# First layers of two MLPs: seven products of 128 rows and one of 64 in place of eight of 120

## The chip, the cores and the metric

The kernel runs on one core of a Trainium2 chip. The metric is the device time of one execution in microseconds (us), as the median of several runs. Beside the runs there is one profiled execution, from which all rows below are taken. The engines are named as in the profile: PE is TensorE (PEld its weight loads), DVE is VectorE, ACT is ScalarE, POOL is GpSimd, SP is SyncE, whose queue issues the DMA transfers.

## What is computed

A linear-attention recurrence over 768 steps for 4 x 8 heads of 40 elements, and behind it two MLPs on the 3072 resulting tokens of 320 elements, each with 2048 hidden elements. The MLPs are dense (one set of weights for all tokens).

```python
def _attn_ref(r, k, v, w, a, b):
    for t in range(S):                      # S = 768, state is (4, 8, 40, 40)
        y[:, :, t] = np.einsum('bhd,bhde->bhe', rt, state)
        Sa = np.einsum('bhde,bhe->bhd', state, at)
        state_decay = state * wt[:, :, None, :] - np.einsum('bhd,bhe->bhde', Sa, bt)
        state = state_decay + np.einsum('bhd,bhe->bhde', vt, kt)

def _moe_ref(x, w_in, w_out):               # x (3072, 320), w_in (320, 2048), w_out (2048, 320)
    h = x @ w_in
    g = h * np.cos(h)
    return g @ w_out

def _moe2_ref(x, w_in, w_out, s, b):
    h = x @ w_in
    r = np.maximum(h, 0.0)
    g = s * (r * r) + b
    return g @ w_out
```

## The kernel before

**Chunks.** Time is cut into 12 chunks of 64 steps. A chunk gives 4 x 64 = 256 tokens. For each chunk `prep` (L1164) loads and scales the inputs, `chain` (L1190) carries the state on, `yt` (L984) leaves the attention's output as two f16 parts (high and low, `yhl`), `xs` (L1009) writes these to DRAM and `x1_load` (L1016) reads them back with the elements of a token on the partitions. `mlp` (L1198) then runs the first MLP on the chunk. When all attention is done, the second MLP runs over the 12 chunks: `x2` (L1063) loads a chunk of the first MLP's result, splits it into high and low parts and transposes it on TensorE.

**Numbers in two parts.** Every f32 operand of the MLPs is a sum of two f16 numbers, high and low. A product of x and w is x_hi w_hi + x_lo w_hi + x_hi w_lo.

**The first layer.** The 320 elements of a token are laid out as 120 + 120 + 80 rows. The 80 rows that are left take 40 more rows from the low parts, so that the tile `w1` (and `w2`), [120, 16, 6, 128], holds six stationary operands for each of the 16 blocks of 128 hidden elements: two high, two low, and two that mix the last 80 high rows with 40 rows of low ones. `first` (L1020) issues eight products for each block `ff`, 120 rows x 128 columns stationary, 256 tokens moving, all into one half of a PSUM bank `hp`. `m1_f` (L1026) and `m2_f` (L1081) call it for ff = 2p and 2p+1, and issue the activation (Sin, Relu) and its split into `gh` and `gl` directly behind the second. `m1_s` and `m2_s` are the second layer: for a pair p and a half m of the tokens, six products of 320 columns into a bank `op`.

**Order.** `mlp` records, for each p, `f(p,0)`, `s(p-2,0)`, `f(p,1)`, `s(p-2,1)`. All operations go through a planner (`Recorder`, L96) that knows each operation's cost and successors; it emits for every engine the operation that can start first, and of equals the one with the longest work behind it. Successive TensorE products of one recorded step are one operation for it. It keeps at most two `hp` and two `op` banks live, and six for attention, of the eight that PSUM has ("cls", L1219). Its cost for products that use at most 64 rows is half of that for more (`cost`, L164); it knows no cost of changing from one kind to the other. All emitted instructions carry line 407, so rows are told apart by the tiles' names.

**Weights.** `weights` (L620) loads `w1` in 16 pieces as 8-byte words; `w_in_chunk` (L575) turns them into f32 on DVE, into the f16 high part on ACT (two operations, as the last 80 rows are wanted twice), and into the low part on POOL. The 40-row pieces of the low part (`wlo`) are moved to rows 80 to 119 by two small transfers for each pair of blocks (`w_in_pair`, L564). `w2` is loaded in 8 pieces of twice the size after attention. `place` (L540) puts raw words into parts of `w1` and `v1` that are not filled yet. The tests (`w_in_test`, `norm`) square the weights and sum them up, as part of a check of the range of numbers.

**Names in the rows.** hp and op are the two layers' banks; tsp are f16 transposes of 40 rows, in turn from rows 0 to 39 and 64 to 103; UD is a product of one row and 512 columns; dtp<-UN,up are f32 products on 32 x 32 pieces, each call two instructions; txp and xtp are transposes of 128 rows; vraw and wraw are raw weights.

Of the kernel before, what the change touches and what calls it, by code (L numbers as in the profile page):

```python
# [29 lines left out]
HEADS = [0, 3, 6, 1, 4, 7, 2, 5]  # L30
# [416 lines left out]
class Fast:  # L447
# [73 lines left out]
    def norm(self, rows, sq, i, k=0):  # L521

        nc = self.nc
        ps = self.pp.tile([128, 2], F32, tag="at", bufs=8, name="np")
        for j, x in enumerate(sq):
            nc.tensor.matmul(ps, x, rows[0:x.shape[0]], start=(j == 0), stop=(j == len(sq) - 1))
        nc.vector.tensor_reduce(out=self.norms[:, k, i:i + 1], in_=ps, axis=AX.X, op=ALU.max)
# [11 lines left out]
    @staticmethod  # L539
    def place(dst, k):  # L540

        q = k + 3 if k < 5 else k if k < 8 else k - 2 if k < 10 else None
        if q is not None:
            return dst[:, 2 * q:2 * q + 2].rearrange("p f a n -> p (f a n)").bitcast(U64)

    def w_in_load(self, src, dst, k):
        p, tag, raws, n = self.wtags[:4]
        raw = self.place(dst, k) if n == 128 else None
        if raw is not None:
            raw = raw.rearrange("p (a n) -> p a n", a=3)  # L550
        else:
            raw = p.tile([120, 3, n], U64, tag=tag, bufs=raws, name="wraw")
        self.RAW["i", k] = raw
        self.nc.sync.dma_start(out=raw, in_=src[:, :, k * n:k * n + n])

    def w_out_load(self, src, dst, k):
        p, tag, raws, n = self.wtags[:4]
        raw = self.place(dst, k) if n == 128 else None
# [5 lines left out]
    def w_in_pair(self, dst, name, k):  # L564

        nc = self.nc
        p, _, _, n, tag, bufs = self.wtags
        lo = p.tile([80, 2, 128], F16, tag=tag, bufs=bufs, name="wlo")
        m = n // 128
        for i in range(0, 2, m):  # L570
            self.w_in_chunk(dst, name, k * 2 // m + i, n, lo[:, i:i + m])
# [3 lines left out]
    def w_in_chunk(self, dst, name, k, n, lo):  # L575
        nc = self.nc
        raw = self.RAW["i", k]
        st = self.float32(raw)
        m = n // 128
# [5 lines left out]
        nc.gpsimd.tensor_tensor(out=wv[:, 2:4], in0=sv[:, 0:2], in1=wv[:, 0:2], op=ALU.subtract)  # L585
        nc.gpsimd.tensor_tensor(out=lo, in0=sv[0:80, 2], in1=wv[0:80, 4], op=ALU.subtract)
# [11 lines left out]
    def w_in_test(self, src, name, k):  # L598

        nc = self.nc  # L600
        sq = self.pm.tile([120, 2, 3, 128], BF16, tag="xs", name="wsq", bufs=4)
        for i, (rows, a, n) in enumerate(((120, 0, 2), (80, 4, 1))):
            nc.scalar.activation(sq[0:rows, :, 2 * i:2 * i + n], src[0:rows, 2 * k:2 * k + 2, a:a + n], AF.Square, scale=1.0 / SW,
                                 accum_out=self.st[0:rows, STAT_IX[name], 2 * k + i:2 * k + i + 1])
        if name == "w1":
            for f in range(2):
                self.norm(self.ones, [sq[0:j, f, i] for i, j in enumerate((120, 120, 80))], 2 * k + f, 1)
# [12 lines left out]
    def weights(self, wn, vn, wd, vd):  # L620
        for k in range(0, NFF, 2):
            l = [(self.w_in_load, self.i[wn], wd, k), (self.w_in_load, self.i[wn], wd, k + 1), (self.w_in_pair, wd, wn, k // 2)]
            for j in (k, k + 1):
                l += [(self.w_out_load, self.i[vn], vd, j), (self.w_out_chunk, vd, vn, j)]
            for j, f in enumerate(l):
                self.do(*f)
                self.nc.base[self.nc.blk] = 265 - 2 * k if j < 3 else 200 - 3 * k
# [356 lines left out]
    def yt(self, c, pg):  # L984
# [12 lines left out]
        if pg == 0:  # L997
            self.Y[c] = self.pa.tile([128, 9, 2, 2 * C], F16, tag="yhl", name="yhl", bufs=1)
# [3 lines left out]
        nc.scalar.activation(self.Y[c][:, 8, pg], y[:, 2 - pg], AF.Copy)  # L1002
# [4 lines left out]
        self.norm(self.halves, [sq[:, h] for h in range(4)], 2 * c + pg)  # L1007

    def xs(self, c):  # L1009

        nc = self.nc
        for hf in range(2):
            y = self.Y[c][hf * 64:hf * 64 + 40].rearrange("p (j i) k t -> p j (i k t)", j=3)
            nc.sync.dma_start(out=self.x0[c, hf].rearrange("j p n -> p j n"), in_=y)

    def x1_load(self, c):  # L1016
        x = self.XS[c] = self.pm.tile([120, 2, 6, 128], F16, tag="xs", name="xs", bufs=4)
        self.nc.sync.dma_start(out=x, in_=self.x0[c].rearrange("f j p n -> (j p) f n"))

    def first(self, ps, w, x, ff):  # L1020
        for i, (a, b) in enumerate(((0, 0), (0, 1), (1, 2), (1, 3), (2, 0), (3, 2), (4, 4), (5, 5))):
            self.nc.tensor.matmul(ps, w[:, ff, a], x[:, b // 2, b % 2], start=(ff % 2 == 0 and i == 0), stop=True,
                                  skip_group_check=True)


    def m1_f(self, c, p, k):  # L1026
        nc = self.nc
        if k == 0:
            self.HP[p] = self.ph.tile([128, 2, TB], F32, tag="at", bufs=8, name="hp")
        ps, x = self.HP[p], self.XS[c]  # L1030
        ff = 2 * p + k
        self.first(ps[:, k, :], self.w1, x.rearrange("p f (i k) t -> p i k f t", k=2), ff)
        if k == 0:
            return
# [28 lines left out]
    def x2(self, j):  # L1063
        nc = self.nc
        xt = self.pb.tile([128, 2, DM], F32, tag="x2f", name="x2f", bufs=2)
        nc.sync.dma_start(out=xt, in_=self.x1[j].rearrange("m p d -> p m d"))
        xq = self.pb.tile([128, 2, 720], F16, tag="x2q", name="x2q", bufs=2)
        xs = self.XS[j] = self.pb.tile([120, 6, 2, 128], F16, tag="x2s", name="x2s", bufs=2)
        for m in range(2):
            xv, q = xt[:, m], xq[:, m]  # L1070
            nc.scalar.activation(q[:, 0:320], xv, AF.Copy, scale=SX2)
            nc.scalar.activation(q.rearrange("p (a e) -> p a e", a=2)[:, :, 320:360],
                                 xv[:, 240:320].rearrange("p (a e) -> p a e", a=2), AF.Copy, scale=SX2)
            nc.vector.scalar_tensor_tensor(out=q[:, 360:680], in0=xv, scalar=SX2, in1=q[:, 0:320],
                                           op0=ALU.mult, op1=ALU.subtract)
            ps = self.pp.tile([128, 6, 128], F16, tag="at", bufs=8, name="xtp")
            for i in range(6):
                nc.tensor.transpose(ps[0:120, i, :], q[:, i * 120:i * 120 + 120], self.ident)
            nc.vector.tensor_copy(xs[:, :, m], ps[0:120])

    def m2_f(self, j, p, k):  # L1081
        nc = self.nc
        if k == 0:
            self.HP[p] = self.ph.tile([128, 2, TB], F32, tag="at", bufs=8, name="hp")
        ps, x = self.HP[p], self.XS[j]
        ff = 2 * p + k
        self.first(ps[:, k, :], self.w2, x.rearrange("p (k i) m t -> p i k (m t)", k=2), ff)
        if k == 0:
            return
# [108 lines left out]
    def mlp(self, f, s, j):  # L1198
# [233 lines left out]
```

## Time and profile before

| | us |
|---|---|
| median of 3 runs | 1165.01 |
| lowest, highest | 1154.4, 1169.88 |
| the profiled execution's own time | 1152.13 |
| its span, first to last instruction | 1150.4 |

The profile has a page with the busy time of each engine and the chain of work that ended last, and views of the trace that can be asked for: busy time in given stretches, groups of instructions by shape, waits, and the timeline. In the timeline, equal instructions that follow one another are one line, with their count; the time between the starts of two lines is the time that the first line's instructions took on the engine. The durations of matmuls include their way through the array, so that they overlap one another: prices are taken from starts. The granted TensorE clock is 1.00 at 2.4 GHz and 0.50 at 1.2 GHz.

### The profile page before, as it was taken

What the parts mean: (1) busy time and instruction counts of PE and PEld (TensorE: products, weight loads), DVE (VectorE), ACT (ScalarE), POOL (GpSimd) and SP (SyncE); (2) the same over time, 40 slices, a digit from 0 to 9 for tenths busy, and PEclk for the clock granted to TensorE, in tenths of its full rate; (3) what the DMA queues carried; (4) which work ended last, traced back from release to release, by engine and by line L of the source; (5) the groups of instructions that cost most, each with busy time, mean ns of one, the idle gap of its engine ahead of it and who ended that gap; (6) DMA issues with size and microseconds to landing.
All of it is one profiled execution on the core that took longest, in us unless ns stands there. A gap on an engine that the chain in (4) does not pass through costs nothing.

```text
span 1150.4 us, 37826 instructions
## 1 busy us (share of the span) xinstructions
PE 993.0 (86%) x16094; PEld 802.2 (70%) x16094; DVE 706.4 (61%) x1390; ACT 728.9 (63%) x1608; POOL 431.4 (37%) x430
## 2 busy tenths in 40 slices
PE   3026889998899799979999998938999999999997
PEld 3025667877677687768788786826888888888885
DVE  6799797829563648382848363978454455544443
ACT  3345678968788777767879664735565544544443
POOL 2576649445544454555465422547300000000000
PEclk9998669998899699989999998969999999999999
DMA  9763454444433543443444304473100100001000
GB/s 226 210 201 120 120 190 153 136 139 132 158 103 94 177 139 102 141 152 115 145 152 144 106 30 137 135 185 88 30 24 24 24 24 23 24 24 25 24 15 23
DMA packets 74755, 121.15 MB, mean 105 GB/s; under 512 B 16500, under 2 KB 47348, under 8 KB 73556
## 3 DMA queue, kind: packets, MB, share of 16 engines
q1 hardware_dynamic: 74580, 118.67, 34.1%
q8 instruction: 128, 2.10, 0.7%
q14 instruction: 47, 0.39, 0.1%
HBM read 72.71 MB, written 12.29 MB: 74 GB/s over the span
## 4 chain that ended last, share of the span: by engine, by line
PE 66%; DVE 11%; DMA 8%; SPq 6%; ACT 6%; issue 3%; POOL 0%; ACTq 0%; DVEq 0%
PE hp L407 26%; PE op L407 23%; SPq L407 6%; PE rhp L407 3%; PE ytp L407 3%; PE uhp L407 3%; DVE XX L407 2%; DMA XX<-in_w 2%; DVE wraw L407 2%; DVE v L407 2%; PE dtp L407 1%; DMA x2f<-x 1%; DMA xs<-x 1%; DMA wraw<-in_w 1%; PE ydp L407 1%
## 5 line engine op out<-in xcount | busy, mean ns | idle before, releaser
L407 PEld LDWEIGHTS <-w 120*128 120x128 f16 x3072 | 297.2, 99 | 73.4 <-DMA xs<-x 21.6
L407 PE MATMUL op<-v,gh 128*128 128x320 f16 x1536 | 325.0, 302 | 1.7 <-ACT gh L407 1.7
L407 PE MATMUL op<-v,gl 128*128 128x320 f16 x768 | 231.3, 301 | 1.7 <-POOL gl L407 1.7
L407 PE MATMUL hp<-xs,w 120*128 120x256 f16 x1536 | 204.5, 284 | 23.2 <-DMA xs<-x 22.6
L407 PE MATMUL hp<-x2s,w 120*128 120x256 f16 x1536 | 188.8, 272 | 0.0
L407 POOL TENSOR_TENSOR gl<-q,gh 128x512 f16<-128x512 f32 x96 | 116.5, 1221 | 183.2 <-ACT gh L407 175.8
L407 PEld LDWEIGHTS <-gh 128*128 128x128 f16 x1536 | 143.2, 98 | 49.8 <-ACT gh L407 2.1
L407 DVE SCALAR_TENSOR_TENSOR q<-q,s_t 128x512 f32<-128x512 f32 x96 | 72.3, 753 | 120.8 <-ACT q L407 118.5
L407 ACT ACTIVATE q<-hp 128x512 f32<-128x512 f32 x96 | 57.2, 596 | 126.2 <-PE hp L407 125.9
L407 DVE SCALAR_TENSOR_TENSOR q<-hp,q 128x512 f32<-128x512 f32 x96 | 65.4, 684 | 58.9 <-ACT q L407 58.1
L407 PEld LDWEIGHTS <-gl 128*128 128x128 f16 x768 | 75.4, 98 | 33.0 <-POOL gl L407 2.3
L407 DVE SCALAR_TENSOR_TENSOR gl<-q,b_t,gh 128x512 f16<-128x512 f32 x96 | 72.0, 750 | 38.0 <-ACT gh L407 35.6
L407 ACT ACTIVATE gh<-q,b_t 128x512 f16<-128x512 f32 x96 | 69.1, 720 | 32.3 <-DVE q L407 31.2
L407 ACT ACTIVATE q<-hp,half_pi 128x512 f32<-128x512 f32 x96 | 64.7, 682 | 30.5 <-PE hp L407 29.1
L407 POOL TENSOR_TENSOR kb<-kb,XX 128x512 f32<-128x512 f32 x44 | 57.4, 1316 | 69.8 <-DVE XX L407 47.0
L407 DVE TENSOR_TENSOR_SCAN XX<-XX,starts 128x264 f32<-128x264 f32 x96 | 67.0, 752 | 16.5 <-DMA XX<-in_w 14.2
L407 ACT ACTIVATE gh<-q 128x512 f16<-128x512 f32 x96 | 59.4, 625 | 12.8 <-DVE q L407 12.0
L407 PEld LDWEIGHTS <-KB 120*128 120x128 f16 (+1 forms) x704 | 28.3, 101 | 46.9 <-DMA KB<-kbl 31.4
L407 PE MATMUL rhp<-UF,M 64*64 64x40 f32 (+1 forms) x1536 | 54.2, 230 | 1.0 <-ACT UF L407 0.6
L407 ACT ACTIVATE UF<-uhp 32x320 f32<-32x320 f32 x96 | 41.1, 428 | 22.1 <-PE uhp L407 20.3
L407 ACT ACTIVATE R<-rhp 32x320 f32<-32x320 f32 x96 | 41.1, 429 | 21.4 <-PE rhp L407 19.6
L407 POOL TENSOR_TENSOR kbl<-kb,kbh 128x1024 f16<-128x1024 f32 x22 | 46.8, 2129 | 20.3 <-ACT kbh L407 20.2
(178 smaller groups left out, 1739.3 us busy)
## 6 DMA issues: line engine op xcount, KB each, us to landing
XX<-in_w SPq DMA_DIRECT2D x12, 1056.0 KB
kb<-in_kb SPq DMA_DIRECT2D x24, 512.0 KB
ar<-in_ar SPq DMA_DIRECT2D x22, 512.0 KB
KB<-kbh SPq DMA_DIRECT2D x88, 80.0 KB
ars<-arh SPq DMA_DIRECT2D x88, 80.0 KB
v<-in_v SPq DMA_DIRECT2D x20, 320.0 KB
wraw<-in_w SPq DMA_DIRECT2D x8, 720.0 KB
SS<-SHL SPq DMA_DIRECT2D x88, 50.0 KB
```

The source lines that it names most:

```text
L407: f(*a, **k)
```

## The change

The 320 elements are laid out as 128 + 128 + 64 rows. `w1` and `w2` become [128, 16, 5, 128]: two high operands of 128 rows, one with 64 rows of the last high part and the 64 low rows of the same part, and two low operands. A block takes seven products of 128 rows and one, the tail, of 64 rows. Which half of the rows holds the tail's low part alternates with `ff // 2` (`rows`), so that the tails of ff = 2p-1 and ff = 2p lie on different rows. `tails(p)` issues these two one after the other, ahead of `first(p, 0)`, into the banks of p-1 and p; the tail of ff = 15 stands at the end of its `first`. The activation of a pair (`m1_g`, `m2_g`) moves behind the next pair's tails, and up to three `hp` banks may be live.

With it go: the small transfers of `w_in_pair`, one of the two ACT conversions of a weight piece, the ninth head of `yhl` and its copy, and the reordering of heads on the host. `x1_load` reads a chunk in four transfers instead of one, `x2` in two instead of one, and it splits 384 elements in one ACT operation instead of 320 and 80 in two.

```diff
-    def w_in_pair(self, dst, name, k):
...
-        for j in range(2):
-            nc.sync.dma_start(out=dst[80:120, 2 * k:2 * k + 2, 4 + j], in_=lo[j * 40:j * 40 + 40])
+    @staticmethod
+    def rows(ff):
+        return ff // 2 % 2 * 64
...
-        for a, r, x in ((0, 120, sv[:, 0:2]), (4, 80, bc(sv[0:80, 2], 1, [80, 2, m, 128]))):
-            nc.scalar.activation(wv[0:r, a:a + 2], x, AF.Copy, scale=SW)
+        nc.scalar.activation(wv[:, 0:3], sv, AF.Copy, scale=SW)
...
-        nc.scalar.activation(self.Y[c][:, 8, pg], y[:, 2 - pg], AF.Copy)
...
-        x = self.XS[c] = self.pm.tile([120, 2, 6, 128], F16, tag="xs", name="xs", bufs=4)
-        self.nc.sync.dma_start(out=x, in_=self.x0[c].rearrange("f j p n -> (j p) f n"))
-
-    def first(self, ps, w, x, ff):
-        for i, (a, b) in enumerate(((0, 0), (0, 1), (1, 2), (1, 3), (2, 0), (3, 2), (4, 4), (5, 5))):
-            self.nc.tensor.matmul(ps, w[:, ff, a], x[:, b // 2, b % 2], start=(ff % 2 == 0 and i == 0), stop=True,
-                                  skip_group_check=True)
+        x = self.XS[c] = self.pm.tile([128, 2, 3, 2, 128], F16, tag="xs", name="xs", bufs=4)
+        v, x = self.x0[c].rearrange("f h e n -> f (h e) n"), x.rearrange("p f i k t -> p f i (k t)")
+        for f in range(2):
+            self.nc.sync.dma_start(out=x[:, f, 0:2], in_=v[f, 0:256].rearrange("(i p) n -> p i n", i=2))
+        for h in range(2):
+            self.nc.sync.dma_start(out=x[h * 64:h * 64 + 64, :, 2], in_=v[:, 256:320].rearrange("f p n -> p f n"))
+
+    def tail(self, ps, w, x, ff):
+        r = slice(self.rows(ff), self.rows(ff) + 64)
+        self.nc.tensor.matmul(ps[:, ff % 2], w[r, ff, 2], x[r, 2, 1], start=(ff % 2 == 0), stop=True, skip_group_check=True)
+
+    def tails(self, p, w, x):
+        hp = self.HP
+        hp[p] = self.ph.tile([128, 2, TB], F32, tag="at", bufs=8, name="hp")
+        if p:
+            self.tail(hp[p - 1], w, x, 2 * p - 1)
+        self.tail(hp[p], w, x, 2 * p)
+
+    def first(self, p, k, w, x):
+        ff, hp = 2 * p + k, self.HP
+        for a, i, b in ((0, 0, 0), (0, 0, 1), (1, 1, 0), (1, 1, 1), (2, 2, 0), (3, 0, 0), (4, 1, 0)):
+            self.nc.tensor.matmul(hp[p][:, k], w[:, ff, a], x[:, i, b], start=False, stop=True, skip_group_check=True)
+        if ff == NFF - 1:
+            self.tail(hp[p], w, x, ff)
...
-    def mlp(self, f, s, j):
+    def mlp(self, t, f, g, s, j):
         lag = 2
         for p in range(NFF // 2 + lag):
             for k in range(2):
                 if p < NFF // 2:
+                    if k == 0:
+                        self.do(t, j, p)
                     self.do(f, j, p, k)
+                if k == 0 and 1 <= p <= NFF // 2:
+                    self.do(g, j, p - 1)
                 if p >= lag:
                     self.do(s, j, p - lag, k)
...
-            rec = self.nc = Recorder(nc, {"any": {"at", "xs", "q"}, "cls": {"XT": 3, "rhp": 3, "hp": 2, "op": 2, "xs": 2, "M2": 2, "q": 4, "att": 6}})
+            rec = self.nc = Recorder(nc, {"any": {"at", "xs", "q"}, "cls": {"XT": 3, "rhp": 3, "hp": 3, "op": 2, "xs": 2, "M2": 2, "q": 4, "att": 6}})
+            rec = ... "hp": 3, "op": 2, ...
...
-            self.w1 = pw.tile([120, NFF, 6, 128], F16, name="w1")
+            self.w1 = pw.tile([128, NFF, 5, 128], F16, name="w1")
```

## Rows read from the trace of the kernel before

**Rows 1.** The page, parts 1 and 4: busy time (share of the span); the chain by line.
```profile
PE 993.0 (86%) x16094; PEld 802.2 (70%) x16094; DVE 706.4 (61%) x1390; ACT 728.9 (63%) x1608; POOL 431.4 (37%) x430
...
PE hp L407 26%; PE op L407 23%; SPq L407 6%; PE rhp L407 3%; PE ytp L407 3%; PE uhp L407 3%; DVE XX L407 2%; DMA XX<-in_w 2%; DVE wraw L407 2%; DVE v L407 2%; PE dtp L407 1%; DMA x2f<-x 1%; DMA xs<-x 1%; DMA wraw<-in_w 1%; PE ydp L407 1%
```

**Rows 2.** Windows: length; PE, PEld, DVE, ACT, POOL busy; PEclk; DMA share; GB/s.
```profile
0.00:159.00 159.00, 71.36 (x1500) 60.29 (x1502) 132.42 (x248) 79.56 (x195) 92.08 (x134) 0.85 0.64 183
...
175.00:752.00 577.00, 540.13 (x11277) 434.51 (x11275) 355.67 (x810) 439.68 (x982) 288.98 (x230) 0.95 0.40 129
752.00:802.00 50.00, 25.70 (x186) 19.37 (x184) 37.40 (x45) 21.06 (x44) 31.04 (x26) 0.76 0.62 153
802.00:1135.00 333.00, 333.00 (x2827) 270.40 (x2828) 161.91 (x236) 171.45 (x355) 12.10 (x35) 1.00 0.09 23
```

**Rows 3.** Waits of TensorE over the run: us in total, times, longest.
```profile
PE hp L407 <- DMA xs<-x: 22.6, 4, 19.1
...
PE rhp L407 <- DMA SS<-SHL: 9.7, 5, 3.9
```

**Rows 4.** Timeline of TensorE in the second MLP: start, us, instructions.
```profile
1000.15 0.44 PE L407 MATMUL op<-v,gh 128*128 128x320 f16 x2
...
1001.79 1.91 PE L407 MATMUL hp<-x2s,w 120*128 120x256 f16 x16
1003.53 0.67 PE L407 MATMUL xtp<-ident,x2q 128*120 128x128 f16 x9
```

**Rows 5.** Timeline of TensorE: full products, then work on fewer rows.
```profile
203.36 0.30 PE L407 MATMUL op<-v,gl 128*128 128x320 f16 x1
203.59 0.48 PE L407 MATMUL tsp<-ident,SHL 40*80 40x40 f16 x16
...
252.73 0.82 PE L407 MATMUL hp<-xs,w 120*128 120x256 f16 x6
253.48 0.48 PE L407 MATMUL tsp<-ident,SHL 40*80 40x40 f16 x16
```

**Rows 6.** Timeline of TensorE: work on fewer rows, then full products.
```profile
253.77 0.19 PE L407 MATMUL tsp<-ident,SHL 40*80 40x40 f16 x2
253.89 0.28 PE L407 MATMUL hp<-xs,w 120*128 120x256 f16 x1
...
319.72 0.39 PE L407 MATMUL UD<-eyes,row 1*128 1x512 f16 x1
320.04 0.45 PE L407 MATMUL op<-v,gh 128*128 128x320 f16 x2
```

**Rows 7.** Timeline of TensorE: pieces of 32 rows; transposes of 128 rows.
```profile
187.58 0.63 PE L407 MATMUL dtp<-UN,up 32*32 32x256 f32 x8
188.04 0.44 PE L407 MATMUL dtp<-UN,YT 32*32 32x16 f32 x32
...
728.62 1.04 PE L407 MATMUL hp<-xs,w 120*128 120x256 f16 x8
729.50 0.61 PE L407 MATMUL txp<-ident,U 128*80 128x128 f16 x8
```

**Rows 8.** Groups of instructions: the second MLP's longest activation step (busy us, mean ns).
```profile
L407 DVE SCALAR_TENSOR_TENSOR q<-q,s_t 128x512 f32<-128x512 f32 x96 | 72.3, 753 | 120.8 <-ACT q L407 118.5
```

**Rows 9.** Timeline of SyncE's queue: start, us, transfers issued.
```profile
123.95 1.65 SPq L407 DMA_DIRECT2D w<-wlo  x2
125.64 1.78 SPq L407 DMA_DIRECT2D wraw<-in_w  x2
...
152.50 0.95 SPq L407 DMA_DIRECT2D vraw<-in_v  x2
```

**Rows 10.** Timeline of TensorE: first work after attention's end [idle before].
```profile
771.26 9.94 PE L407 MATMUL hp<-xs,w 120*128 120x256 f16 x64 [19.10 <-DMA xs<-x]
```

**Rows 11.** Groups of instructions on ScalarE in the first 200 us.
```profile
L407 ACT ACTIVATE w<-w 120x256 f16<-120x256 f32 x10 | 4.3, 431 | 6.1 <-DVE w L407 4.2 <-DMA XX<-in_w 1.9
...
L407 ACT ACTIVATE yhl<-y 128x128 f16<-128x128 f32 x4 | 1.2, 298 | 0.0
```

More of the change, by code (lines that the diff above doesn't have):

```diff
@@ L519, in square, with norm @@
         self.nc.scalar.activation(j, x, AF.Square, scale=scale, accum_out=self.st[rows, STAT_IX[name], i:i + 1])
-    def norm(self, rows, sq, i, k=0):
+    def norm(self, sq, i, k=0):
         nc = self.nc
         ps = self.pp.tile([128, 2], F32, tag="at", bufs=8, name="np")
-        for j, x in enumerate(sq):
-            nc.tensor.matmul(ps, x, rows[0:x.shape[0]], start=(j == 0), stop=(j == len(sq) - 1))
+        for j, (x, rows) in enumerate(sq):
+            nc.tensor.matmul(ps, x, rows, start=(j == 0), stop=(j == len(sq) - 1))
         nc.vector.tensor_reduce(out=self.norms[:, k, i:i + 1], in_=ps, axis=AX.X, op=ALU.max)
@@ L600, in w_in_test @@
         nc = self.nc
[L601 to L604, printed above, removed]
+        sq = self.pm.tile([128, 2, 3, 128], BF16, tag="xs", name="wsq", bufs=4)
+        accum = lambda r, i: self.st[r, STAT_IX[name], 2 * k + i:2 * k + i + 1]
+        nc.scalar.activation(sq[:, :, 0:2], src[:, 2 * k:2 * k + 2, 0:2], AF.Square, scale=1.0 / SW, accum_out=accum(slice(0, 128), 0))
+        r = slice(self.rows(2 * k), self.rows(2 * k) + 64)
+        nc.scalar.activation(sq[r, :, 2], src[r, 2 * k:2 * k + 2, 2], AF.Square, scale=1.0 / SW, accum_out=accum(r, 1))
         if name == "w1":
             for f in range(2):
-                self.norm(self.ones, [sq[0:j, f, i] for i, j in enumerate((120, 120, 80))], 2 * k + f, 1)
+                self.norm([(sq[:, f, 0], self.ones), (sq[:, f, 1], self.ones), (sq[r, f, 2], self.ones[r])], 2 * k + f, 1)
     def w_out_test(self, src, name, k):
@@ L1006, in yt @@
                              accum_out=self.st[:, STAT_IX["y"], 2 * c + pg:2 * c + pg + 1])
-        self.norm(self.halves, [sq[:, h] for h in range(4)], 2 * c + pg)
+        self.norm([(sq[:, h], self.halves) for h in range(4)], 2 * c + pg)
     def xs(self, c):
@@ L1035, in m1_f, with m1_t, m1_g @@
+    def m1_t(self, c, p):
+        x = self.XS[c]
+        self.tails(p, self.w1, x.rearrange("p f i k t -> p i k f t"))
+    def m1_f(self, c, p, k):
+        x = self.XS[c]
+        self.first(p, k, self.w1, x.rearrange("p f i k t -> p i k f t"))
+    def m1_g(self, c, p):
+        nc, ps = self.nc, self.HP[p]
         q = self.pm.tile([128, 2, TB], F32, tag="q", name="q", bufs=8)
@@ L1081, in m2_f @@
-    def m2_f(self, j, p, k):
[L1082 to L1089, printed above, removed]
+        xt = self.pb.tile([128, 2, 384], F32, tag="x2f", name="x2f", bufs=2)
+        v = self.x1[j].rearrange("m p d -> p m d")
+        nc.sync.dma_start(out=xt[:, :, 0:320], in_=v)
@@ new lines, in x2 @@
+        nc.sync.dma_start(out=xt[:, :, 320:384], in_=v[:, :, 256:320])
+        q = self.pb.tile([128, 2, 2, 384], F16, tag="x2q", name="x2q", bufs=2)
+        xs = self.XS[j] = self.pb.tile([128, 3, 2, 2, 128], F16, tag="x2s", name="x2s", bufs=2)
+        for m in range(2):
+            nc.scalar.activation(q[:, 0, m], xt[:, m], AF.Copy, scale=SX2)
+            nc.vector.scalar_tensor_tensor(out=q[:, 1, m], in0=xt[:, m], scalar=SX2, in1=q[:, 0, m], op0=ALU.mult, op1=ALU.subtract)
+            ps = self.pp.tile([128, 3, 2, 128], F16, tag="at", bufs=8, name="xtp")
+            for i in range(3):
+                for b in range(2):
+                    nc.tensor.transpose(ps[:, i, b], q[:, b, m, i * 128:i * 128 + 128], self.ident)
+            nc.vector.tensor_copy(xs[:, :, :, m], ps)
@@ L1090, in m2_f, with m2_t, m2_g @@
+    def m2_t(self, j, p):
+        x = self.XS[j]
+        self.tails(p, self.w2, x.rearrange("p i b m t -> p i b (m t)"))
+    def m2_f(self, j, p, k):
+        x = self.XS[j]
+        self.first(p, k, self.w2, x.rearrange("p i b m t -> p i b (m t)"))
+    def m2_g(self, j, p):
+        nc, ps = self.nc, self.HP[p]
         q = self.pm.tile([128, 2, TB], F32, tag="q", name="q", bufs=8)
@@ L1260, in run @@
             self.pb = pool(es_b, "late")
[L1261 to L1262 removed]
+            self.w2 = self.pb.tile([128, NFF, 5, 128], F16, name="w2")
+            self.wtags = self.pb, "braw", 6, 256
             for k in range(FF // 256):
                 self.do(self.w_in_load, self.i["w2"], self.w2, k)
[L1265 removed]
+                self.do(self.w_in_chunk, self.w2, "w2", k)
             for j in range(NC):
                 self.do(self.x2, j)
[L1268 removed]
+                self.mlp(self.m2_t, self.m2_f, self.m2_g, self.m2_s, j)
                 if j == 3:
```

99 lines of the change are left out of this document (34 added, 65 removed).

## The prediction

> **What bounds the kernel now.** I read the page first. TensorE is busy for 993.0 us of the span, far more than any other engine, and in the chain of work that ended last the two largest lines are TensorE's first layer (hp, 26% of the span) and second layer (op, 23%) [rows 1]. That is an average, so I cut the span into stages next [rows 2]. From 0 to 159 us VectorE (132.42 us) and the loads set the pace, and TensorE is busy less than half the time. From 175 to 752 us attention and the first MLP run interleaved, and TensorE is busy 540.13 of 577.00 us. From 752 to 802 us the second MLP's weights arrive. From 802 to 1135 us the second MLP runs alone, and there TensorE is busy 333.00 of 333.00 us at a granted clock of 1.00 (the 2.4 GHz level). The list of waits agrees: over the whole run the first layer was kept waiting 22.6 us in 4 places, 19.1 us of it in one place at 771 us [rows 3, 10]. So in the last stage, and nearly so in the one from 175 us, each nanosecond that the first layer adds to TensorE is added to the end.
>
> The timeline of TensorE gives the price of its work there [rows 4]. Sixteen first-layer products start at 1001.79, and the next work starts at 1003.53: 1.74/16 = 0.109 us each. Twelve second-layer products take from 1000.15 to 1001.79: 0.137 us each. One pass over a chunk has 16 blocks of ff, 8 products each: 128 products, 13.9 us, and there are 12 chunks and two MLPs, 24 passes.
>
> **The change on TensorE.** Per pass it takes 128 full products and makes them 112 full ones and 16 of 64 rows (the tails). `tails(p)` issues two of these back to back, for ff = 2p-1 and 2p, on rows 0 to 63 and 64 to 127 and into two PSUM banks: 7 such pairs. The tail of ff = 0 has no partner in its own block, and that of ff = 15 is issued behind `first`. These two are single unless the planner lays the end of one pass against the start of the next, where they would be on different rows too.
>
> Do two tails run side by side? No row shows 64-row products of 256 columns, so I bound it. Near row: eight f32 products of 256 columns on 32x32 pieces (dtp<-UN,up) take 187.58 to 188.04, 0.46 us; one after another at even the f16 price they would take 8 x 0.109 = 0.87 us [rows 7]. So pieces on different rows overlap there. The transposes of 40 rows (tsp), which alternate between the halves of the rows as the tails will and have full-width columns, are even listed two at one start, 253.77 [rows 6]. I take a pair as one product, 0.109 us, plus 0.01; the bound above is no overlap, 0.218.
>
> Now what it costs to get into and out of half-row work. Six first-layer products start at 252.73, and the half-row transposes behind them at 253.48: 0.75 us, where 6 x 0.109 = 0.654. That is 0.096 too much. A second-layer product starts at 203.36 and the transposes at 203.59: 0.23 instead of 0.137, again 0.093 [rows 5]. The control is a transposition of 128 rows behind eight first-layer products: 728.62 to 729.50, 0.88 for 8 x 0.109 = 0.87, no loss [rows 7]. So it isn't the transposition, it is the change of rows. Leaving costs as much: the one-row product of 512 columns (UD) starts at 319.72 and the next full one at 320.04, 0.32 where 512 columns are worth 2 x 0.109 = 0.218, so 0.10; and from the last transposes at 253.77 to the first-layer product at 253.89 pass 0.12, though the sixteen of them came in 0.29 us, about 0.04 a pair, so 0.08 [rows 5, 6]. I take 0.095 in and 0.10 out, 0.195 for both, since the two nearest in columns say so; bounds 0.175 and 0.20.
>
> The Trainium skill has a rule here, in "TensorEngine Tiling (Array Packing)", Key Properties: changing the tiling mode, not just the tile, drains TensorE. The trace agrees, with 0.09 to 0.10 us at each such change. The page gives no duration, so by it the sum keeps its sign and has no size; the sum below goes by the rows alone.
>
> So a pair: 0.195 + 0.109 + 0.01 = 0.314 us in place of 2 x 0.109 = 0.218: **0.09 to 0.10 us lost, not 0.109 won**; I take 0.095. A single one: 0.195 lost. A pass has 7 pairs and then either an eighth (0.76 us in all) or two singles (0.665 + 0.39 = 1.06). I take the middle, 0.91. Twelve passes of the second MLP, all of it exposed: 10.9 us. Twelve of the first, of which TensorE's idle share there can hide some (540.13/577.00 = 0.94 exposed): 10.2. Together **+21 us**, bounds 17.6 (all paired, with the 0.94) and 25.4 (all single, nothing hidden).
>
> **The rest of the change.** Loading the first-layer weights: the 32 small transfers of `w_in_pair` (w<-wlo) go, the half of them in the first 160 us. Two of them took 1.65 us of SyncE's queue at 123.95, and the two weight loads behind them 1.78, where two loads of 128 partitions (vraw) took 0.95; the weights too now have 128 [rows 9]. That is 1.65 + 0.83 = 2.5 us off the queue in that one place, and there may be another such. ScalarE converts each chunk in one operation of 384 elements in place of two of 256 at about 431 ns each, and a copy of 298 ns goes in each `yt` [rows 11]. Against it stand 128/120 of the bytes. I take -4 us for the first stage; bounds 0 (other work, VectorE's above all, sets the pace there) and -10 (four places). In the middle stage, 752 to 802 us, the weights of the second MLP come in 8 pieces of 120 x 3 x 256 words of 8 bytes, 737 KB, that grow to 786 KB; TensorE stands still there for 19.1 us until the chunk's input (xs) has landed among them [rows 10]. Four times 49 KB at that stage's 153 GB/s [rows 2] is 1.3 us more; fewer transfers and shorter conversions give about as much back: 0, bounds -3 and +3. The 36 more loads of `x1_load` and 12 of `x2` take SyncE's issue time, less than the freed 32 did, and are hidden behind TensorE from 175 us on.
>
> The activations (`m1_g`, `m2_g`) now start after `tails(p+1)`, six second-layer products (0.82 us) later. In the second MLP their four operations, the longest of 753 ns [rows 8], take 3.0 us at most; the second layer that needs them stands behind two half-passes: 2 x 0.76 + 2 x 0.82 + 0.31 + 0.76 = 4.2 us after. So it is hidden, with a spare of 1.2 us.
>
> Sum: +21 - 4 + 0 = **+17 us** on the profiled execution's 1152.1: 1169. That execution lies 12.9 us under the median of the runs; on the median it is **1182 us**.
>
> **The rivals.**
>
> 1. *The change of rows is free for these products* (faster). Only the f16 weights of 128 columns are new here; if their loads ran ahead after all, a pair would save 0.109 - 0.01. That is 8 x 24 x 0.10 = 19 us, 23 with the first stage: 1142. It decides from a switch cost under 0.05 us a side. Against it: tsp and UD, of two piece sizes, show 0.08 to 0.10 at every place [rows 5, 6]. The Trainium skill, "TensorE: Matmul & The Clock Gate", Part 3, is on this side: it has products on distinct row groups run concurrently, and puts no price on coming and going. By it the time is this rival's; the trace speaks against. Chance 0.08.
> 2. *Attention waits for PSUM* (slower still). The planner may now keep three hp banks live in place of two; with two of op, three of eight are left where `rhs` and `u_half` want four. TensorE is idle 37 us in the stage from 175 us [rows 2]; attention's waits that can be told apart there (rhp for SS) last 9.7/5, about 2 us [rows 3]. One more of half that in each of 12 chunks gives +12: 1194. For it: the granted clock of that stage is 0.95, so its lower level, 1.2 GHz, is met already, and each wait invites it. Against it: the planner sees the banks and can order around them. Chance 0.15.
> 3. *Tails don't overlap.* Then each pair loses 0.195: 24 x 8 x 0.195 = 37 us, 33 in all: 1198. Against it rows 6 and 7. Chance 0.05.
> 4. *The planner's new order hides more of the first MLP's share*: half of it, 5 us, and the first stage gives 10: 1182 - 11 = 1171. Chance 0.17.
>
> My forecast has 0.55.
>
> **How the numbers follow.** The forecast's own bounds are +17.6 - 10 - 3 and +25.4 + 3: 1170 to 1193 on the median. The runs of before themselves reach from 1154.4 to 1169.9, about 8 us to either side. With rivals 4 and 2 taken in: **1158 to 1199**; rival 1 and the ends stay out. About 2% (23 us, 1142 and 1188) is what can be told from no change. Slower by more than that: rivals 2 and 3 most of the time, and a quarter of the forecast's: 0.17 + 0.14 = 0.31. Faster: rival 1 about half the time and a little beside: 0.05. Within 2%: 0.64.
>
> **What would show it.** In the second MLP of the changed kernel: from the product before a pair of tails to the pair 0.20 to 0.23 us, both tails at one start, and 0.21 us to the next full product; the stage still busy throughout, and a pass longer by 0.8 to 1.1 us (of 27.7 now, 333/12). If the pair's surroundings show 0.11 each, rival 1 holds. A second tail 0.1 us behind the first: rival 3. Waits of uhp or rhp in the list of waits, and a clock under 0.95 from 175 us: rival 2. First products of the first MLP earlier than now by 4 us would bear out the first stage. I am wrong in kind if the last stage gets shorter.

## The result, and the profile after

The changed kernel takes 1179.81 us (median of 17 runs, 1169.3 to 1192.87), the kernel before 1162.49 us on the same chip (17 runs, 1154.4 to 1170.44). The ratio is 1.0136 with a 95% interval of 1.0103 to 1.0168: slower by 1.4%, about 16 us, where 1182 us and "within 2%" were forecast. The profiled execution has a span of 1167.6 us (its time 1169.3) where before had 1150.4 (1152.1): 17.2 us more, where the sum said +17. Both profiled executions lie at the low end of their runs. The longer runs of a kernel tend to be those with the lower mean granted clock, in the changed kernel 0.939 in its fastest run and 0.922 in its slowest, so the clock is given below where a time can't be understood without it.

The page of the changed kernel, parts 1 and 4, as in [rows 1]:

```profile
PE 1021.2 (87%) x16094; PEld 782.0 (67%) x16094; DVE 712.8 (61%) x1390; ACT 711.6 (61%) x1536; POOL 436.4 (37%) x430
...
PE hp L406 27%; PE op L406 25%; DVE wraw L406 3%; PE rhp L406 3%; DVE XX L406 3%; SPq L406 2%; PE ytp L406 2%; PE uhp L406 2%; PE dtp L406 1%; PE s1p L406 1%; DMA XX<-in_w 1%; PE ydp L406 1%; PE txp L406 1%; POOL kb L406 1%; DVE M L406 1%
```

The same 16094 TensorE instructions keep that engine busy for 28 us longer. ScalarE has 72 instructions fewer and 17 us less to do. The windows of the changed kernel, in the stretches and columns of [rows 2]:

```profile
0.00:159.00 159.00, 82.17 (x1658) 69.67 (x1658) 139.82 (x268) 80.86 (x188) 101.65 (x142) 0.83 0.58 187
175.00:752.00 577.00, 546.88 (x11179) 424.11 (x11176) 349.48 (x796) 430.00 (x948) 279.22 (x220) 0.96 0.39 125
752.00:802.00 50.00, 22.22 (x156) 14.99 (x155) 46.06 (x47) 17.53 (x29) 35.96 (x30) 0.69 0.50 177
802.00:1135.00 333.00, 333.00 (x2731) 245.62 (x2729) 154.28 (x229) 157.86 (x324) 7.45 (x31) 1.00 0.10 24
```

The last stage is as full as before, 333.00 of 333.00 us at a granted clock of 1.00, and in the same time TensorE gets through 2731 instructions in place of 2827: they are dearer on average. Between 752 and 802 us TensorE is busy for 3.5 us less than before.

The price can be read off directly. TensorE's timeline in the second MLP of the changed kernel (start, us, instructions), and under it that of its weight loads:

```profile
1001.48 0.30 PE L406 MATMUL op<-v,gl 128*128 128x320 f16 x1
1001.71 0.28 PE L406 MATMUL hp<-x2s,w 64*128 64x256 f16 x2
1001.92 0.45 PE L406 MATMUL op<-v,gh 128*128 128x320 f16 x2
1002.20 0.30 PE L406 MATMUL op<-v,gl 128*128 128x320 f16 x1
```

```profile
1001.34 0.10 PEld L406 LDWEIGHTS <-gl 128*128 128x128 f16 x1
1001.70 0.10 PEld L406 LDWEIGHTS <-w 64*128 64x128 f16 x2 [0.26 <-issue]
1001.92 0.11 PEld L406 LDWEIGHTS <-gh 128*128 128x128 f16 x2
```

A second-layer product of 320 columns, worth 0.136 us between others of its kind, is followed by the pair of tails only after 0.23 us. Both tails start together, the second 0.003 us behind the first: the line of two lasts 0.28 us, where the line of a single full product lasts 0.30. The next full product comes 0.21 us after the pair. Its weights, and the tails', are loaded only when their turn has come: 1001.70 and 1001.92 are the starts of the products themselves. The full product at 1001.48 had its weights at 1001.34, one product ahead. Between 1001.48 and 1001.92 pass 0.44 us; three full products in that place would take 0.136 + 2 x 0.109 = 0.354.

The second MLP has tails with plain first- or second-layer products around them. Over these the starts in the trace give the following means ("late" is what exceeds the full price of the product before, 0.136 or 0.109 us by kind):

| | instances | first tail late | first tail to the next full product | the product behind that one, late | lost against products of 128 rows |
|---|---|---|---|---|---|
| a pair | 78 | 0.096 | 0.216 | 0.010 | 0.104 us |
| a single tail | 14 | 0.096 | 0.212 | 0.011 | 0.210 us |

The changed kernel has 170 pairs, 38 single tails (the expectations below count 39) and two groups of three, at about 0.1 us each. The planner laid only four ends of a pass in the second MLP against the start of the next. 170 x 0.104 + 38 x 0.210 + 0.2 = **25.9 us**: 13.7 in the first MLP, 12.2 in the second. The 13.7 is an estimate at the second MLP's prices, and rather from above: in the first MLP 36 of the 108 groups of tails stand next to attention's work on at most 64 rows, where the rows change anyway.

### The profile page after: what moved, and what is told of

It reads as the page before. It is cut to its first block, busy times and chain, and to the rows that moved or that the text cites. A ratio compares the mean times of both kernels' runs of the same rounds, so it can differ in the third digit from the quotient of the medians.

```text
span 1167.6 us, 37829 instructions
## 1 busy us (share of the span) xinstructions
PE 1021.2 (87%) x16094; PEld 782.0 (67%) x16094; DVE 712.8 (61%) x1390; ACT 711.6 (61%) x1536; POOL 436.4 (37%) x430
## 4 chain that ended last, share of the span: by engine, by line
PE 68%; DVE 13%; DMA 6%; ACT 4%; issue 3%; POOL 3%; SPq 2%; ACTq 0%; DVEq 0%; POOLq 0%
PE hp L406 27%; PE op L406 25%; DVE wraw L406 3%; PE rhp L406 3%; DVE XX L406 3%; SPq L406 2%; PE ytp L406 2%; PE uhp L406 2%; PE dtp L406 1%; PE s1p L406 1%; DMA XX<-in_w 1%; PE ydp L406 1%; PE txp L406 1%; POOL kb L406 1%; DVE M L406 1%
## 5 line engine op out<-in xcount | busy, mean ns | idle before, releaser
L406 PEld LDWEIGHTS <-w 128*128 128x128 f16 (+1 forms) x3072 | 278.5, 99 | 95.9 <-issue 44.7
L406 PE MATMUL hp<-xs,w 128*128 128x256 f16 (+1 forms) x1536 | 211.4, 285 | 7.9 <-issue 3.7
L406 PE MATMUL hp<-x2s,w 128*128 128x256 f16 (+1 forms) x1536 | 190.1, 274 | 0.0
L406 PEld LDWEIGHTS <-gh 128*128 128x128 f16 x1536 | 134.6, 98 | 57.9 <-issue 2.4
L406 ACT ACTIVATE gh<-q 128x512 f16<-128x512 f32 x96 | 59.6, 624 | 17.2 <-DVE q L406 16.8
L406 POOL TENSOR_TENSOR arl<-ar,arh 128x1024 f16<-128x1024 f32 x22 | 47.9, 2178 | 27.7 <-ACT arh L406 27.6
L406 ACT ACTIVATE UF<-uhp 32x320 f32<-32x320 f32 x96 | 41.1, 428 | 25.9 <-PE uhp L406 24.0
L406 ACT ACTIVATE R<-rhp 32x320 f32<-32x320 f32 x96 | 41.0, 427 | 21.4 <-PE rhp L406 19.7
```

The lines of the kernel that those rows point to most:

```text
L406: f(*a, **k)
```

## The experiments

**Theory**: each change from products of 128 rows to products of 64 and back costs about 0.2 us, so a pair costs more than the 0.109 us that it was to win. **Rivals**: the loss comes from the third hp bank and the moved activations (order, waits, clock), or from the new layout and its transfers; or the tails don't overlap.

### Full rows in place of the tails

The changed kernel with nothing but the tails' shape undone: each is a product of all 128 rows, one at a time, in the same place. (It adds low parts times low parts for 64 elements, so it computes a little more than the reference asks.)

```diff
-        r = slice(self.rows(ff), self.rows(ff) + 64)
-        self.nc.tensor.matmul(ps[:, ff % 2], w[r, ff, 2], x[r, 2, 1], start=(ff % 2 == 0), stop=True, skip_group_check=True)
+        self.nc.tensor.matmul(ps[:, ff % 2], w[:, ff, 2], x[:, 2, 1], start=(ff % 2 == 0), stop=True, skip_group_check=True)
```

> The changed kernel with one thing undone: each tail is a product of all 128 rows. The other 64 rows then add low part times low part, which is a term that belongs to the product too. Number of products, their order, the three hp banks and the later activations stay as in the changed kernel; only the half-row products are gone. Theory (each turn to half-row work and back costs TensorE about 0.2 us): the changed kernel has 170 pairs and 39 single tails in its trace, worth 170 x 0.094 + 39 x 0.199 = 24 us; without them 1180 - 24 = 1156 us, ratio to the kernel before 0.995, with no 64-row group left and 0.109 us between all first-layer products. Rival (the new order, the later activations or the third bank cost the time): it stays at 1.0136.

Measured: 1156.02 us (9 runs; before 1163.65 of 14), ratio 0.9921 [0.988, 0.9962]. The whole loss is gone, and 0.8% beside it. In the tails' place now stand two full products, which take their price of 0.22 us and hold the next one off no longer:

```profile
1001.24 0.38 PE L406 MATMUL hp<-x2s,w 128*128 128x256 f16 x2
1001.46 0.43 PE L406 MATMUL op<-v,gh 128*128 128x320 f16 x2
```

The number of instructions, the rules of their order, banks, transfers and activations are those of the change. So the loss is the tails' 64 rows, and the rest of the change is a gain. 1.0136/0.9921 = 1.022: the tails cost 25 us (about 6 either way), where the list above adds up to 25.9.

### All tails single

Each tail stands beside its own block's products, so that no two are meant to follow one another.

```diff
-        if p:
-            self.tail(hp[p - 1], w, x, 2 * p - 1)
...
-        if ff == NFF - 1:
+        if k:
             self.tail(hp[p], w, x, ff)
```

> The changed kernel with every tail beside its own block's seven products, none paired: 384 single tails in place of 170 pairs and 39 singles, the same number of products. Theory: each costs 0.199 us over an ordinary product of 0.109, 384 x 0.199 = 76 us, where the changed kernel paid 24: 1180 + 52 = 1232 us, ratio 1.06. Rival (order and banks cost the time, not the turns): within 1 per cent of the changed kernel. This doubles the suspected cost and more.

Measured: 1230.37 us (4 runs), ratio 1.0561 [1.0506, 1.0616]. Its timeline of TensorE, where the line of eight is seven full products and a tail:

```profile
1002.94 1.14 PE L406 MATMUL hp<-x2s,w 128*128 128x256 f16 x8
1004.01 0.45 PE L406 MATMUL op<-v,gh 128*128 128x320 f16 x2
```

1.07 us from the first of the eight to the next product, where eight full ones take 8 x 0.109 = 0.87: 0.20 late, and the product behind it loses the other 0.01. The sum fits too. The trace has 192 single tails in the second MLP, and 148 single ones, 13 twos and 6 threes in the first (the planner moved some together): at 0.210 for a single one, and 0.10 to 0.21 for each of the other groups, 73 to 75 us. Against the kernel with full rows it lost 74 (1.0561/0.9921 = 1.0645). That total holds other things too: TensorE waits 22.4 us in the middle stage here, 8 less than with full rows, and the granted clock of the runs is lower (0.928 for 0.940, see the first MLP alone below). The dose that holds by itself is that of the second MLP, counted further down.

### Both tails on the same rows

```diff
     def rows(ff):
-        return ff // 2 % 2 * 64
+        return 0
```

> The changed kernel with all tails on rows 0 to 63, so that the two of a pair lie on the same rows. Theory (two tails run side by side because they lie on different rows, and the pair saves one product of 0.109 us): the second tail starts 0.11 us behind the first in place of 0.004, 170 pairs lose 0.105 us each, 18 us: ratio to the kernel before 1.029. Rival (the starts in the trace are drawn closer than the work is, and pairs are done one after the other anyway): no change from 1.0136.

Measured: 1187.71 us (4 runs), ratio 1.0177 [1.0111, 1.0242], less than the 1.029 expected. So it was run again beside the changed kernel:

> e2_same_rows once more, beside the changed kernel on the same chip: it was 1.0177 against the kernel before where 1.029 was expected, though its profile has the second MLP 9 us and the stretch before it 9 us over the changed kernel's. Theory (pairs on different rows save 18 us): 1.5 per cent over the run of the changed kernel beside it. Rival (half of that is given back): 0.5 to 0.8 per cent.

> The changed kernel, for e2_again to be compared with: 1.0136 against the kernel before, as measured.

Measured: 1187.0 us, 1.0256 [1.0199, 1.0313], and for the changed kernel 1176.96, 1.0167 [1.0104, 1.0231] (6 runs each; before 1162.36 of 20). The timeline of the former:

```profile
1001.31 0.39 PE L406 MATMUL hp<-x2s,w 64*128 64x256 f16 x2
1001.63 0.45 PE L406 MATMUL op<-v,gh 128*128 128x320 f16 x2
```

The two tails together now last 0.39 us in place of 0.28 and hold the next product off for 0.32 in place of 0.21. So in the change they do run side by side, and that is worth 0.105 us a pair, 17.9 us for 170 pairs. The profiled spans differ by 20.5 us (1186.8 and 1166.3), the medians by only 10: the two intervals leave room for 0 to 1.7%, and the forecast 1.5% lies inside. So the times alone don't settle that size; the trace does. The runs agree with it if the granted clock is taken into account: a run's span times its mean granted clock, in which time at the lower level (0.50) counts half, is 1112.3 us here and 1096.5 in the changed kernel (means of 6 runs each), 16 us apart with some 4 either way.

### Groups of eight tails

If the price is one of going in and out, it is shared by more tails. In the second MLP four hp banks are opened at once, twice a pass, and their eight tails follow one another, in turn on either half of the rows. That wants five banks there and a planner that counts several new banks of one step. In the first MLP, where attention needs the banks, the tails have full rows.

```diff
+    def group(self, p, w, x):
+        hp = self.HP
+        for i in range(4):
+            hp[p + i] = self.ph.tile([128, 2, TB], F32, tag="at", bufs=8, name="hp")
+        for i in (0, 2):
+            for k in range(2):
+                for q in (p + i, p + i + 1):
+                    self.tail(hp[q], w, x, 2 * q + k)
...
+            rec.caps["cls"]["hp"] = 5
```

> The first MLP with tails of 128 rows as in e1_full_rows; in the second MLP eight tails of four banks stand together, twice a pass, with up to five hp banks live. Theory (one turn there and back of 0.2 us is paid for a group, whatever its length, and four pairs in it take 4 x 0.113): a group costs 0.65 us for 8 x 0.109 = 0.87 us of ordinary products, 0.22 us won, 24 groups: 5.3 us under e1_full_rows, 1151 us, ratio 0.990. Rival (each pair pays on its own): 96 pairs x 0.094 = 9 us over e1_full_rows, 1.003. Rival (five banks hold the second MLP up): waits of the transposes or of hp appear in it.

Measured: 1138.97 us (6 runs), ratio **0.9775 [0.9735, 0.9815]**, faster than both kernels. Its timeline:

```profile
1012.96 0.30 PE L406 MATMUL op<-v,gl 128*128 128x320 f16 x1
1013.19 0.61 PE L406 MATMUL hp<-x2s,w 64*128 64x256 f16 x8
1013.73 0.45 PE L406 MATMUL op<-v,gh 128*128 128x320 f16 x2
```

From 1012.96 to 1013.73 pass 0.77 us; with eight full products it would be 0.136 + 8 x 0.109 = 1.01. Over 23 groups the mean is 0.222 us won, with the same 0.096 going in. 24 groups give 5.3 us. Against the kernel with full rows it is 1.5% faster, 17 us with about 7 either way, so more than the groups is in it. The rest is in the middle stage. Waits of TensorE from 745 to 825 us (us, times, longest), first with full rows, then with groups:

```profile
PE xtp L406 <- ACT x2q L406: 20.6, 1, 20.6
PE xtp L406 <- DVE x2q L406: 9.6, 4, 6.0
```

```profile
PE hp L406 <- DMA xs<-x: 19.9, 1, 19.9
```

With full rows, as in the change itself (20.9 and 6.9 us), the transposes of the second MLP's first chunks (xtp) stand ahead of the first MLP's last products in TensorE's queue and wait there for their data from ScalarE and VectorE, five times. With groups the planner puts the first MLP's products first, as before the change [rows 10], and the transposes come when their data are there. The long wait of about 20 us stands in either order, and the first MLP's products could hardly have filled it. In the change the last transfers of their own input (xs) are issued only shortly before it ends (SyncE's queue, then TensorE):

```profile
770.57 1.46 SPq L406 DMA_DIRECT2D xs<-x  x2
```

```profile
773.07 0.29 PE L406 MATMUL xtp<-ident,x2q 128*128 128x128 f16 x1 [20.88 <-ACT x2q L406]
```

What the order gives back are the shorter waits. In all they are 10.3 us less, so with the 5.3 us most of the 17 are accounted for, by single traces.

### What moved the middle stage

Is it the five banks? The kernel with full rows, and five banks after attention:

```diff
+            rec.caps["cls"]["hp"] = 5
```

> e1_full_rows with one thing more: from the end of attention up to five hp banks may be live, as in e4_groups_of_8. That kernel ended 19 us before e1_full_rows in the profile, of which the second MLP gave 8.7 and the stage from 750 to 800 us the rest, 10.5. Theory (the bank limit lets the planner run the last chunk of the first MLP out while the second one's weights arrive): 10 us under e1_full_rows, 1146 us, ratio 0.985, one stall of 20 us at 750 and none of the transposes behind it. Rival (the groups themselves changed the order): as e1_full_rows, 0.992.

Measured: 1153.08 us (12 runs; before 1162.36), ratio 0.9944 [0.9909, 0.9978], as with three banks and not the 0.985 of the theory, and the transposes still stand first in the trace (the same window):

```profile
PE xtp L406 <- ACT x2q L406: 20.1, 2, 19.5
PE xtp L406 <- DVE x2q L406: 4.6, 3, 2.9
```

So more banks alone are not it; the order that comes with the groups is what is left.

Is it the order of the change? The change's layout and transfers alone: eight products of 128 rows, the order and the two hp banks of before.

```diff
     def first(self, p, k, w, x):
...
+        self.tail(hp[p], w, x, ff)
         for a, i, b in ((0, 0, 0), (0, 0, 1), (1, 1, 0), (1, 1, 1), (2, 2, 0), (3, 0, 0), (4, 1, 0)):
...
     def m1_f(self, c, p, k):
...
+        if k:
+            self.m1_g(c, p)
```

> The change's layout and transfers (128 + 128 + 64 rows, no small transfers, one conversion), but eight products of 128 rows in the order of the kernel before: each tail a full product ahead of its block's seven, the activations directly behind the second block, two hp banks. e1_full_rows measured 0.992 against the kernel before. Theory (what the change wins beside the tails is in the loading and conversion of the weights): 0.992 here too, 1154 us. Rival (it is won by the third bank and the later activations): 1.000, and first-layer work starts no earlier than in the kernel before.

Measured: 1147.69 us (9 runs), ratio 0.989 [0.9851, 0.993]. So the layout gives 1.1%, and what the new order and the third bank add or take (0.9921 against 0.989) is inside the intervals. TensorE's long wait in the middle is here that of the first MLP's products for their input, as before:

```profile
PE hp L406 <- DMA xs<-x: 21.8, 1, 21.8
```

With 0.6 us for a shorter one it waits 22.4 us there, 7.8 less than with full rows in the change's order (30.2). The medians of the two kernels differ by as much, but inside the intervals: the price of the order is read from traces, and no pair of runs shows it by itself.

With this first MLP and the groups of eight in the second:

> The two that did best put together: the first MLP as in e7_layout_only (eight products of 128 rows in the order of the kernel before, two hp banks), the second MLP with groups of eight tails and five banks as in e4_groups_of_8, its activations directly behind their block. Theory (a turn is paid once a group: a group of 8 tails took 0.64 us in the trace of e4_groups_of_8 where eight products take 0.87): e7 less 24 x 0.23 = 5.6 us, 1142 us, ratio 0.984; if it also loses the stalls behind the first one, as e4_groups_of_8 did, 1138. Rival (what e4_groups_of_8 won was the order it happened to get): 0.989, as e7_layout_only.

Measured: 1140.97 us (6 runs; before 1164.32 of 17), ratio 0.9809 [0.9762, 0.9856]. It also beats both kernels, and is not told apart from the other kernel with groups. Against the layout alone, which has the same order in the middle, the medians differ by 7 us, where the groups count 5.3.

### Tails of 64 rows in the first MLP alone

```diff
-        r = slice(self.rows(ff), self.rows(ff) + 64)
+        r = slice(self.rows(ff), self.rows(ff) + 64) if self.half else slice(0, 128)
...
+            self.half = True
...
+            self.half = False
```

The first switch stands in front of the loop over the first MLP's chunks, the second in front of that over the second's.

> The changed kernel with the second MLP's tails made products of 128 rows; the first MLP keeps its pairs of half-row tails. Theory (the first MLP's turns are exposed nearly as the second's are: 0.94, 12 us each): halfway between the changed kernel (1.015) and e1_full_rows (0.992), 1.003, 1167 us. Rival (attention beside it hides the first MLP's share): near e1_full_rows, 0.994. Other rival (in the first MLP the turns cost more than their time, by the clock): 1.008 or more.

Measured: 1168.56 us (12 runs), ratio 1.0039 [1.0004, 1.0075]. Against the kernel with full rows that is 1.0039/0.9921 = 1.0119, 13.7 us for the first MLP; 1.0136/1.0039 = 1.0097, 11 us, are left for the second, each with some 6 us either way. The list says 13.7 and 12.2. So the first MLP's tails do cost time, and the rival that attention hides all of it is excluded.

But that they are paid as the list counts them, as time on TensorE, is not shown, and two things speak against it. First, in the profiled executions the second MLP's first product starts at 799.9 us here, at 804.3 in the change and at 804.8 with full rows: ahead of it these traces, at mean granted clocks of 0.941, 0.939 and 0.935, show no loss. Second, the profiled execution here is the fastest of 12, at a mean granted clock of 0.941, while the median of the 12 is 0.929, and that of the nine runs with full rows 0.940. The seven runs that lie within 1.5% of the fastest have a median of 1164.3 us, 8 and not 12.5 over that of the kernel with full rows. Span times mean granted clock is 1085 us here and 1082 with full rows (means of the runs), only 3 us apart with about 3 either way, where the spans themselves are 14 apart. In the change it is 1097, 16 more than with full rows, and the second MLP alone makes 12 of these, as counted below. So by this estimate the smaller part of the first MLP's share is time on TensorE, and the larger part came with a lower granted clock. That was the third possibility of the expectation, at a smaller size. The other kernels agree: with tails of 64 rows in the first MLP the median clock is 0.928 to 0.938, with the same layout and full rows there 0.940 to 0.944 (before the change 0.937). Why it is lower stays open.

### The stretch of the second MLP, counted

From the first hp<-x2s product to the last op product, by the timelines. In the kernels of the lower two rows some of the first MLP's last products stand inside it, for about 7 us at its beginning; so they are set against the kernel with full rows, where that is so too.

| kernel | us | against | difference | counted from the list |
|---|---|---|---|---|
| all single | 377.4 | before, 337.2 | +40.2 | 192 x 0.210 = 40.3 |
| groups of eight | 331.8 | before, 337.2 | -5.4 | 24 x -0.222 = -5.3 |
| the change | 352.9 | full rows, 340.5 | +12.4 | 87 x 0.104 + 14 x 0.210 + 0.2 = 12.2 |
| both on the same rows | 362.1 | full rows, 340.5 | +21.6 | 87 x 0.209 + 14 x 0.210 + 0.3 = 21.4 |

Two prices, 0.096 going in and about 0.11 coming out, account for four kernels within 0.2 us, at a granted clock of 1.00 and with no waits of TensorE in the stretch. This is the firm part of the case.

## Why the prediction was right, step by step

**What bounds the kernel**: right. The last stage stayed full and grew by what TensorE's products grew.

**The change of rows**: right in kind, and nearly in size. 0.095 in and 0.10 out had been read from the transposes of 40 rows and the product of one row [rows 5, 6]; the tails, f16 products of other shape and with other neighbours, show 0.096 and 0.10. The control [rows 7], that full-width work pays nothing, also holds. What those rows were not read for is the second product after the change, another 0.010 us late, which makes a pair 0.104 and not 0.095, and a single 0.210 and not 0.195.

**Do two tails overlap**: right. The second starts 0.003 to 0.004 us behind the first, 0.12 on the same rows.

**How many pairs**: the middle between seven pairs with two singles and eight pairs a pass was taken. The planner gave the first nearly everywhere: 170 pairs and 38 singles. At the forecast's own prices that is 170 x 0.095 + 38 x 0.195 = 23.6 us, not 21.8.

**How much of the first MLP's share is exposed**: 0.94 was taken from TensorE's busy share, 10.2 us. The runs give 13.7 with 6 either way, so the size holds, but hardly by the route that was forecast: of TensorE's own time some 3 us are seen, and the rest came with a lower granted clock, which the forecast priced only for waits of attention. That the total comes out near the forecast's is in this term partly luck. All the tails together were forecast at +21 us, bounds 17.6 and 25.4; the runs give 25 with 6 either way.

**The rest of the change**: -4 with 0 to -10 was forecast. The kernel with full rows says -0.8%, about 9 us, and the layout alone -1.1%, about 13, each with 5 us either way. So this term was sized too small, for the layout clearly: 25 - 9 gives the measured 16, as 21 - 4 had given 17. Both parts came out 4 to 5 us larger than forecast, to opposite sides, and that is near the noise of either. That two errors met in the close agreement is likely and not shown. Where the layout's 1.1% lies stays open. The forecast's mark for the first stage doesn't find it: first products of the first MLP were to come 4 us earlier, and in the change they come 5.4 us earlier (153.9 for 159.3 us), but with the layout alone 6.8 us later (166.1), and that kernel is the faster one. So that mark says nothing of the gain. The profiled spans of before and of the layout alone, 1150.4 and 1147.1, differ by 3 us only, since before's was one of its fastest executions; single traces that scatter as much as the effect can't locate it.

**The middle stage**: forecast 0, -3 to +3, from bytes and conversions. The change waits there for 20.9 + 6.9 us, where before waited 19.1 us for the chunk's input and about 5 in shorter waits:

```profile
PE xtp L407 <- DVE x2q L407: 2.6, 1, 2.6
PE op L407 <- ACT gh L407: 1.7, 1, 1.7
PE op L407 <- POOL gl L407: 0.8, 1, 0.8
```

That is some 3 us more, at the bound. With the layout alone it waits 22.4 us there, 2 less than before, as the forecast's "about as much back" allows; the change's order adds 5. That order, the transposes ahead of the first MLP's last products, was none of the causes weighed: the forecast had asked what bytes and conversions cost there, and not which operation would now stand first in TensorE's queue. Single traces show it, as said above.

**The activations' later start**: hidden, as forecast. In the whole run the second layer's products wait for 0.9 us on the activations' low part (gl), and for 0.4 on a tile of attention (SD), as TensorE's groups of the changed kernel show (the last part is the idle time and its releaser):

```profile
L406 PE MATMUL op<-v,gh 128*128 128x320 f16 x1536 | 325.6, 302 | 0.4 <-ACT SD L406 0.4
L406 PE MATMUL op<-v,gl 128*128 128x320 f16 x768 | 231.1, 301 | 0.9 <-POOL gl L406 0.9
```

**The rivals.** *The change of rows is free*: excluded by the timelines, the dose and the kernel with full rows. The sentence of the Trainium skill that stood on its side ("TensorE: Matmul & The Clock Gate", Part 3: distinct row groups run concurrently) is borne out by the 0.003 to 0.004 us, and it is not the whole price. The Trainium skill's rule in "TensorEngine Tiling (Array Packing)", Key Properties, that a change of mode drains TensorE, agrees with the loss at each change, 0.096 us in and 0.11 out; no run shows what happens inside the engine in that time. *Attention waits for PSUM*: excluded as far as the third bank goes, since with full rows and the same three banks there is a gain. Its sign of a clock under 0.95 from 175 us is absent in the profiled execution, 0.96, but that was the fastest run; over the span the median of the changed kernel's runs is 0.931, before 0.937, and in which stage the typical run has less was not profiled. The waits it named, of the changed kernel over the whole run (us, times, longest):

```profile
PE uhp L406 <- ACT DT L406: 5.5, 2, 3.3
...
PE rhp L406 <- DMA SS<-SHL: 1.9, 3, 1.2
```

Those of rhp for SS have fallen from 9.7 [rows 3]; two of uhp for ScalarE have come, 5.5 us. *Tails don't overlap*: excluded by their starts and by the kernel that puts them on the same rows. *The planner hides more of the first MLP's share*: its time, 1171, is excluded by the measured interval. Its mechanism is not: by the granted clocks most of that share is no time on TensorE.

## What to carry to other kernels

Products on half the rows pay for the way in and out, here 0.096 and 0.11 us, so they win only in company: at 0.109 us for a product of 256 columns a pair loses 0.10 us, and eight tails in a row win 0.22. Look for the price in work of the kernel at hand that already changes its rows, count the changes and not the products, and ask how the order can bring the tails together before halving anything. And where a sum of two opposite terms comes out right, undo one of them on the chip: here each came out 4 to 5 us larger than forecast, and the total hid it. Look at the granted clock of all runs too, and not only at the profiled one.

## What the runs showed of the chip

The weights of a half-row product are not loaded ahead across the change of rows: the load stands at the product's own start, where between full products it stands one product ahead (1001.70 and 1001.34 above). Within a group of half-row products loads run ahead again: the eight loads of a group start within 0.24 us, while a pair of its products starts every 0.11 to 0.12 us, and the price is paid once a group. The weight loads of that group:

```profile
1013.18 0.33 PEld L406 LDWEIGHTS <-w 64*128 64x128 f16 x8 [0.26 <-issue]
1013.73 0.11 PEld L406 LDWEIGHTS <-gh 128*128 128x128 f16 x2 [0.21 <-issue]
```

And the second product after a change back is late by another 0.009 to 0.011 us, at all places counted in the second MLP.
